# A fused attention and SwiGLU kernel: work behind group 0's first blocks ordered from a job list, more products by sevens

## The chip, the cores and the metric

The kernel runs on one core of one Trainium2 chip. The metric is device time in microseconds (us) from launch to the last store, the median of three runs. TensorE (PE) multiplies matrices into PSUM, a memory of eight banks of 2 KB a partition; VectorE (DVE) and ScalarE (ACT) read and write PSUM and SBUF; GpSimd (POOL) and SyncE (SP) issue the DMAs here.

## The reference

```python
# B, H, S, D = 8, 8, 576, 64; x is 4608 x 512; w_gate, w_val 512 x 1536; w_out 1536 x 512
theta = pi / 2 * arange(S) / S
phi = lambda x: concat([relu(x) * cos(theta), relu(x) * sin(theta)], -1)
kv = einsum('bhsf,bhsd->bhfd', phi(k), v); z = phi(k).sum(axis=2)
attn = einsum('bhsf,bhfd->bhsd', phi(q), kv) / (einsum('bhsf,bhf->bhs', phi(q), z) + 1e-6)
x = attn.transpose(0, 2, 1, 3).reshape(4608, 512)
out = (silu(x @ w_gate) * (x @ w_val)) @ w_out
```

Linear attention without a mask, whose output goes straight into a gated feed-forward layer. All inputs and the output are float32.

## The kernel before

The 4608 tokens are 36 tiles of 128, and nine groups (tg 0 to 8) of 512 tokens. The hidden width 1536 is twelve blocks of 128 (fc 0 to 11). Attention of later batches runs among the feed-forward work of earlier groups.

*Attention.* Loads are issued on POOL (L149), some behind a small copy (a hold) that keeps the queue until a tile is there. For a batch from 2 on, relu and the tables give the features of q (L301) and the weighted v (L311), SP transposes q's features in two DMAs (`phit`, L330), PE makes kv (L361) into a pair of banks, and DVE and ACT take it out (L387, L393). A tile of x (`a_tile2`, L492) is eight products into a pair of banks; then DVE computes den (L506), rec (L515) and x (L519) from both banks. Tiles 4 to 8 are computed as two half tiles (`a_half`, L542): PE fills a pair of banks, ACT makes `tmp` (L552) from both, DVE `num` (L553) from both and tmp. x is transposed by an SP DMA (L596), tiles 6 and 7 by PE.

*Feed-forward.* A plain block (`ffn_fc`) is four 512-column products for the gate and four for val (L612), silu on ACT (L618) and the product of both on DVE (L623). In groups 5 to 8 (`GATE`) the gate is computed for four blocks at a time (a unit u = 0, 1, 2) by seven products of half size in place of eight, after Strassen and Winograd (`ffn_by_quarters`, L670), from weight sums (L645) and sums of x (L653); ACT copies two partial results (L699, L703) and DVE adds two (L709, L718). The out product of groups 1 to 8 is made by seven products in the same way (`out_by_quarters`, L846 with L859 to L887), from sums of tokens (L818) and of weights (L809). Group 0's out product is plain (L787), in pieces of four 512-column products.

*Order.* Every engine works in the order in which its instructions were written. That order is a list of words up to group 0's early blocks, and behind it a plan of slots filled by hand from tables (`ROW`, `TILES`, `LATER`, `LATE`). PSUM is one tile of eight banks; `take(n)` gives one bank or two, a pair being neighbours:

```python
b0 = sorted((b for b in free if b + 1 in free), key=lambda b: max(used[b:b + 2]))
bs = [b0, b0 + 1]
return banks[:, bs[0]] if n == 1 else banks[:, bs[0]:bs[0] + 2]
```

Waits between engines are derived when the kernel is built from what each instruction reads and writes.

Of the kernel before, what the change touches and what calls it, by code (L numbers as in the profile page):

```python
# [18 lines left out]
def kernel(  # L19
# [10 lines left out]
    nc = tc.nc  # L30
# [21 lines left out]
    GATE = (5, 6, 7, 8)  # L52
    AHEAD = 5
    WSUM = (31, 38, 48, 64)
    ROW = {2: ([16, 16, 17, 17], 18, (20, 21, 21, 22), 8), 3: ([12, 12, 14, 14], 18, (17, 20, 21, 21), 6), 4: ([12, 12, 12, 14], 14, (15, 16, 17, 18), 5), 5: ([12, 12, 12, 14], 15, (14, 16, 16, 17), 4), 6: ([6, 8, 11, 12], 12, (13, 14, 15, 18), 3), 7: ([6, 6, 7, 7, 8, 8, 9, 9, 10, 10, 11, 11, 12, 12, 13, 13, 14, 14], 16, (12, 13, 14, 15), 3)}
    TILES = {2: (0, 9, 10, 11), 3: (5, 9, 10, 11), 4: (5, 7, 9, 11), 5: (3, 4, 7, 9), 6: (0, 2, 5, 7), 7: (0, 1, 5, 7), 8: (0, 3, 5, 7)}
    SECOND = (31, 37, 38, 79)
    TSUM = [(2, 2), (2, 3), 18, 19]
    KVONE = (2, 4, 5)
    LATER = {2: (0, 1, 3, 4, 7, 8), 3: (0, 1, 3, 4, 7, 8), 4: (0, 1, 3, 4, 7, 8), 5: (0, 1, 3, 4, 7, 8), 6: (0, 1, 3, 4, 7, 8), 7: (0, 1, 3, 4, 7, 8), 8: (0, 1, 3, 4, 7, 8)}  # L60
    LATE = dict(M=44, V=87, O=131, X=26, x=150, v=(190, 250, 120, 150), e=130, a=90, c=170, b=110, k=120)

    consts = ctx.enter_context(tc.tile_pool(name="consts", bufs=1))
    raw = ctx.enter_context(tc.tile_pool(name="raw", bufs=2))
# [3 lines left out]
    xp = ctx.enter_context(tc.tile_pool(name="xp", bufs=4))  # L68
    xtp = ctx.enter_context(tc.tile_pool(name="xtp", bufs=3))
    smp = ctx.enter_context(tc.tile_pool(name="smp", bufs=3))  # L70
    sgp = ctx.enter_context(tc.tile_pool(name="sgp", bufs=5))
    sg2p = ctx.enter_context(tc.tile_pool(name="sg2p", bufs=3))
    m7p = ctx.enter_context(tc.tile_pool(name="m7p", bufs=2))
    obp = ctx.enter_context(tc.tile_pool(name="obp", bufs=2))
# [10 lines left out]
    filled = [False] * 8  # L85
    loose = [False]
    picks = [0]
    rows = [0]

    def take(n, hold=None, fills=False, seeded=False):  # L90

        taken = {x for r in held.values() for x in r}
        if loose[0]:
            free = [b for b in range(8) if b not in taken]
            picks[0] += 1
            other = picks[0] in SECOND
            if n == 1:
                bs = sorted((b for b in free if filled[b] or not seeded), key=lambda b: used[b])
                bs = bs[min(other, len(bs) - 1):][:1]
            else:  # L100
                b0 = sorted((b for b in free if b + 1 in free), key=lambda b: max(used[b:b + 2]))
                b0 = b0[min(other, len(b0) - 1)]
                bs = [b0, b0 + 1]
            if hold is not None:
                held[hold] = bs
            for b in bs:
                filled[b] = fills or seeded
            touch(bs)
            return banks[:, bs[0]] if n == 1 else banks[:, bs[0]:bs[0] + 2]
        free = [b for b in range(0, 8, n) if not any(b <= x < b + n for x in taken)  # L110
                and (filled[b] or not seeded)]

        b0 = min(free, key=lambda b: (n == 1 and hold is not None and hold[0] == "o" and b ^ 1 not in taken,
                                      sorted(used[b:b + n], reverse=True)))
        if hold is not None:
            held[hold] = range(b0, b0 + n)
        filled[b0:b0 + n] = [fills or seeded] * n
        touch(range(b0, b0 + n))
        return banks[:, b0] if n == 1 else banks[:, b0:b0 + n]

    def touch(r, late=1):
        now[0] += 1
        if loose[0]:
            for x in r:
                used[x] = rows[0] + late
            return
        for x in r:
            used[x] = now[0]

    def give_back(hold, late=1):  # L130
        touch(held.pop(hold), late)


    raws = {}
# [5 lines left out]
    def raw_of(b, nm):  # L140
        if (b, nm) not in raws:
            raws[b, nm] = (rawq if nm == "q" else raw).tile([P, G, NC, D], BF16, name=f"raw_{nm}")
        return raws[b, nm]
# [151 lines left out]
    def phi_q(b, g):  # L295

        if g == 0:
            st[b, "q"] = rel.tile([P, G, NC, 2, D], BF16, name="r_q")
        o = raws[b, "q"][:, g]
        relu_op("act", o, o)  # L300
        nc.vector.tensor_tensor(out=st[b, "q"][:, g], in0=o.unsqueeze(2).to_broadcast([P, NC, 2, D]),  # L301
                                in1=tab, op=ALU.mult)

    def phi_q_part(b, c, w):
        if (b, "q") not in st:
            st[b, "q"] = rel.tile([P, G, NC, 2, D], BF16, name="r_q")
        nc.scalar.activation(out=st[b, "q"][:, :, c, w], in_=raws[b, "q"][:, :, c], func=AF.Relu,
                             scale=csk[:, c, w:w + 1])

# [17 lines left out]
    def qturn_dma(b, e):  # L327
        if e == 0:
            phit[b] = phip.tile([P, 2, G, NC, SH], BF16, name="phit")
        nc.sync.dma_start_transpose(  # L330
            out=phit[b][:, e].rearrange("p g c s -> p (g c) s"),
            in_=st[b, "q"][e * SH:(e + 1) * SH].rearrange("p g c w d -> p (g c w d)"),
        )

# [8 lines left out]
    def qturn_pe(b, j, lo, hi, eng):  # L343
        ps = take(1).bitcast(BF16).rearrange("p (c x) -> p c x", x=P)
        for c in range(lo, hi):
            nc.tensor.transpose(out=ps[:, c - lo], in_=st["qp"][:, b, c, j], identity=ident)
        copy_op(eng, qt_of(b)[:, :, j, lo:hi].rearrange("p e c s -> p c e s"),
                ps[:, 0:hi - lo].rearrange("p c (e s) -> p c e s", e=2))

    def kv_mm(b):  # L350
        if b in KVONE:
            ps = st[b, "kvps"] = [take(1, ("kv", b, e)) for e in range(2)]
        else:
            both = st[b, "kvps"] = take(2, ("kv", b))
            ps = [both[:, e] for e in range(2)]
        for j, c in [(j, c) for j in range(J) for c in range(NC)]:
            for i in range(2):
                for e in range(2):
                    es = slice(e * SH, (e + 1) * SH)
                    g = 2 * j + i  # L360
                    nc.tensor.matmul(  # L361
                        out=ps[e][i * D:(i + 1) * D, j * 2 * D1:(j + 1) * 2 * D1],
                        lhsT=raws[b, "k"][es, g, c],
                        rhs=v2s[b == 1][es, g, c, :, 0:D1],
                        start=(c == 0), stop=(c == NC - 1),
                    )

    def kv_out(b, engs=("act", "dve"), js=slice(0, J)):
        ps = st[b, "kvps"]
        for e, eng in enumerate(engs):  # L370
            for i in range(2):
                hs = slice(i * D, (i + 1) * D)
                (nc.scalar.copy if eng == "act" else nc.vector.tensor_copy)(
                    out=kvd[b % 2][hs, e, js, :, i].rearrange("p j w x -> p (j w) x"),
                    in_=ps[hs, e, js.start * 2 * D1:js.stop * 2 * D1].rearrange("p (y x) -> p y x", x=D1))

    behind = []
    kv2s = [consts.tile([P, 2, J, 2, D1], BF16, name=f"kv2_{j}") for j in range(2)]

    def kv_out2(b):  # L380

        if b in KVONE:
            for e, eng in enumerate((nc.scalar.copy, nc.vector.tensor_copy)):
                ps = st[b, "kvps"][e][:, 0:4 * J * D1 // 2].rearrange("p (j w x) -> p j w x", j=J, w=2)
                for w in range(2):
                    for i in range(2):
                        eng(out=kv2s[b % 2][w * D:(w + 1) * D, e, :, i], in_=ps[i * D:(i + 1) * D, :, w])  # L387
                give_back(("kv", b, e))
            return
        ps = st[b, "kvps"][:, :, 0:4 * J * D1 // 2].rearrange("p e (j w x) -> p e j w x", j=J, w=2)  # L390
        def part(w, eng):
            for i in range(2):
                eng(out=kv2s[b % 2][w * D:(w + 1) * D, :, :, i], in_=ps[i * D:(i + 1) * D, :, :, w])  # L393

        part(0, nc.scalar.copy)
        if b - 1 in GATE:
            behind.append(lambda: (part(1, nc.vector.tensor_copy), kv_free(b)))
        else:
            part(1, nc.vector.tensor_copy)

    def kv_free(b):
        give_back(("kv", b), LATE["k"])

    def kv_first(j, lo=0, hi=NC):

        if lo == 0:
# [96 lines left out]
    def x_den(t, ps, ys=slice(0, 4)):  # L503
        if ys.start == 0:
            st["den", t] = smp.tile([P, H, 1], FP32, name="den")
# [655 lines left out]
```

## Time and profile before

| what | value |
|---|---|
| time, median of 3 runs | 311.84 us (311.62 to 312.58) |
| span of the profiled execution | 309.8 us; its own time is not given apart, the median lies 2.04 us above the span |
| TensorE busy | 302.2 us of the span, mean granted clock 0.999 |
| DVE, ACT, POOL busy | 240.9, 155.5, 67.7 us |
| groups 0 to 8 end at about | 54, 86.6, 119, 151.3, 183.9, 215.4, 246.7, 276.4, 305.2 us |
| from group 8's last product to the end | 4.6 us |

A share of the span is an average. The windows, busy time of each engine between two moments, show it group by group. The list of waits says for how long an engine stood still before an instruction, and which engine's instruction released it. In a timeline the figure in square brackets at a line's end is the idle time before it.

### The profile page before, as it was taken

Reading aid. Unit: us, or ns where it says so; the run is one execution under the profiler, and the core shown is the slowest. Engines: PE = TensorE matmul, PEld = TensorE weight load, DVE = VectorE, ACT = ScalarE, POOL = GpSimd, SP = SyncE. Lnnn points to the kernel's source line nnn. Section 1 sums busy time; section 2 is a strip of 40 time slices with the busy share of each in tenths; the row PEclk is TensorE's granted clock in tenths of the full one; section 3 lists DMA queues with packets and bytes.
Section 4 is the critical chain, followed back from the end, with each engine's and each line's share of the span. In section 5 each row is a group of like instructions: output and inputs, shape, how many; then the busy total and the mean of one; then the engine's idle time right before and its main releaser. Section 6 shows DMA issues by size and latency. Waiting matters only on the chain.

```text
span 309.8 us, 7026 instructions
## 1 busy us (share of the span) xinstructions
PE 302.2 (98%) x2804; PEld 200.5 (65%) x2804; DVE 240.9 (78%) x486; ACT 155.5 (50%) x297; POOL 67.7 (22%) x119
## 2 busy tenths in 40 slices
PE   8899999999999999999999999999999999999993
PEld 4587465445855486547654686768766876786683
DVE  7874678999877988687888887898789569855782
ACT  7454646674355355435644455778553345324530
POOL 7755202001250306030413032202300130031000
PEclk9999999999999999999999999999999999999999
DMA  7999998996499899949696999991991051013005
GB/s 264 222 198 197 206 205 142 227 139 110 72 221 186 129 172 146 202 70 196 123 191 85 200 122 142 126 167 22 179 133 31 14 140 35 19 47 91 0 0 139
DMA packets 72977, 41.10 MB, mean 133 GB/s; under 512 B 49904, under 2 KB 69872, under 8 KB 72944
## 3 DMA queue, kind: packets, MB, share of 16 engines
q0 software_dynamic: 24880, 24.91, 47.0%
q1 hardware_dynamic: 47616, 15.34, 30.8%
q8 instruction: 22, 0.36, 0.5%
q10 hardware_dynamic: 448, 0.39, 0.4%
q14 instruction: 11, 0.09, 0.1%
HBM read 37.75 MB, written 9.44 MB: 152 GB/s over the span
## 4 chain that ended last, share of the span: by engine, by line
PE 92%; DVE 5%; ACT 2%; issue 1%; DVEq 0%; ACTq 0%
PE banks L612 31%; PE banks L846 24%; PE banks L683 13%; PE banks L670 12%; PE banks L787 3%; PE banks L492 2%; PE banks L361 2%; DVE v L311 1%; PE banks L542 1%; PE banks L473 1%; PE banks L215 1%; DVE ht L623 1%; PE banks L416 0%; PE banks L584 0%; ACT L247 0%
## 5 line engine op out<-in xcount | busy, mean ns | idle before, releaser
L618 ACT ACTIVATE sg<-banks 128x512 bf16<-128x512 f32 (+2 forms) x68 | 37.2, 548 | 49.8 <-PE banks L612 49.3
L612 PE MATMUL banks<-xT,wg_sb 128*128 128x512 f16 (+2 forms) x272 | 62.0, 354 | 0.0
L612 PE MATMUL banks<-xT,wv_sb 128*128 128x512 f16 (+2 forms) x272 | 62.0, 354 | 0.0
L623 DVE TENSOR_TENSOR ht<-sg,banks 128x512 f16<-128x512 bf16 (+2 forms) x68 | 41.7, 621 | 17.7 <-PE banks L612 11.8
L769 POOL DMA_DIRECT2D out_dram<-ob x56 | 29.5, 534 | 101.0 <-ACT ob L859 99.2
L683 PE MATMUL banks<-xT,wv_sb 128*128 128x512 f16 x192 | 48.6, 379 | 0.0
L612 PEld LDWEIGHTS <-wv_sb 128*128 128x128 f16 x272 | 26.1, 98 | 26.1
L846 PEld LDWEIGHTS <-ht 128*128 128x128 f16 x384 | 37.4, 98 | 5.4
L612 PEld LDWEIGHTS <-wg_sb 128*128 128x128 f16 x272 | 24.9, 98 | 21.4
L688 DVE TENSOR_TENSOR ht<-sg,banks 128x512 f16<-128x512 bf16 x48 | 31.0, 681 | 3.3 <-ACT sg L676 3.1
L846 PEld LDWEIGHTS <-sums 128*128 128x128 f16 x288 | 28.2, 98 | 3.3
L683 PEld LDWEIGHTS <-wv_sb 128*128 128x128 f16 x192 | 18.8, 98 | 13.3
L676 ACT ACTIVATE sg<-banks 128x512 bf16<-128x512 f32 x36 | 20.5, 590 | 11.8 <-PE banks L670 11.8
L846 PE MATMUL banks<-wo_sb,ht 128*128 128x256 f16 x192 | 23.6, 273 | 0.0
L519 DVE TENSOR_TENSOR x<-banks,rec 128x512 f16<-128x512 f32 (+1 forms) x32 | 21.6, 675 | 1.3 <-PE banks L473 0.3
L670 PEld LDWEIGHTS <-wgs_sb 128*128 128x128 f16 x192 | 17.8, 98 | 7.4 <-issue 0.6
L846 PE MATMUL banks<-wt_sb,ht 128*128 128x256 f16 x192 | 22.3, 273 | 0.0
L846 PE MATMUL banks<-wt_sb,sums 128*128 128x256 f16 x192 | 22.3, 273 | 0.0
L670 PE MATMUL banks<-kvt,wgs_sb 128*128 128x256 f16 x144 | 21.6, 273 | 0.4 <-DVE x L519 0.4
L311 DVE TENSOR_TENSOR v<-raw_v,tab 128x1152 bf16<-128x1152 bf16 x27 | 19.8, 754 | 0.4 <-ACT raw_v L909 0.4
L859 ACT ACTIVATE ob<-banks 128x512 f32<-128x512 f32 x15 | 9.0, 598 | 21.9 <-PE banks L846 21.9
L301 DVE TENSOR_TENSOR r_q<-raw_q,tab 128x1152 bf16<-128x1152 bf16 x20 | 14.4, 754 | 5.1 <-ACT raw_q L284 4.7
(126 smaller groups left out, 411.8 us busy)
## 6 DMA issues: line engine op xcount, KB each, us to landing
out_dram<-ob POOLq DMA_DIRECT2D x56, 128.0 KB, 4.8
raw_k<-in_k_dram POOLq DMA_DIRECT2D x7, 576.0 KB, 6.7
raw_q<-in_q_dram POOLq DMA_DIRECT2D x6, 576.0 KB, 9.0
raw_v<-in_v_dram POOLq DMA_DIRECT2D x6, 576.0 KB, 9.6
wo_sb<-in_moe_w_out_dram POOLq DMA_DIRECT2D x3, 512.0 KB, 12.8
out_dram<-ob SPq DMA_DIRECT2D x12, 128.0 KB, 4.1
wg_sb<-in_moe_w_gate_dram POOLq DMA_DIRECT2D x5, 256.0 KB, 9.0
wv_sb<-in_moe_w_val_dram POOLq DMA_DIRECT2D x5, 256.0 KB, 9.2
```

Source lines behind the costliest of these rows:

```text
L301: nc.vector.tensor_tensor(out=st[b, "q"][:, g], in0=o.unsqueeze(2).to_broadcast([P, NC, 2, D]), in1=tab, op=ALU.mult)
L311: nc.vector.tensor_tensor(out=v2s[b == 1][:, g, :, :, 0:D], in0=(first if b == 0 and g == 0 else {"v": raw_of(b, "v")})["v"][:, g].unsquee ...
L519: nc.vector.tensor_tensor(out=st["x", t].rearrange("p (y e d) -> p e y d", e=2, d=D)[:, :, ys], in0=ps[:, :, 0:2 * J * D1].rearrange("p e ...
L612: nc.tensor.matmul(out=st["f", tg, fc, lo][i], lhsT=(wg_sb, wv_sb)[i][:, kc, fs], rhs=xT[tg][:, ts, kc], start=(kc == 0), stop=(kc == KC - 1))
L618: nc.scalar.activation(out=sg[:, 0:n], in_=st["f", tg, fc, lo][0], func=AF.Silu, scale=DOWN)
L623: nc.vector.tensor_tensor(out=ht[:, fc, r:r + n], in0=st.pop(("s", tg, fc, lo))[:, 0:n], in1=ps[1], op=ALU.mult)
L670: nc.tensor.matmul(out=to[:, i], lhsT=a[:, c, 2 * u + i], rhs=x[:, :, c], start=first and i == 0 and c == 0, stop=c == KH - 1, skip_group_ ...
L676: nc.scalar.activation(out=gates[u, w][:, :, j * HT:(j + 1) * HT], in_=src, func=AF.Silu, scale=DOWN)
L683: nc.tensor.matmul(out=val[u, i, w], lhsT=wv_sb[:, kc, fc * P:(fc + 1) * P], rhs=xT[tg][:, :, kc], start=(kc == 0), stop=(kc == KC - 1))
L688: nc.vector.tensor_tensor(out=ht[:, fc], in0=gates[u, w][:, i], in1=val.pop((u, i, w)), op=ALU.mult)
L769: (queues or (nc.sync, nc.sync))[e].dma_start(out=out_v[idx // NC, idx % NC][:, cols], in_=ob_of(t)[e * SH:(e + 1) * SH, cols])
L846: nc.tensor.matmul(out=to[i][:, 0] if len(to) == 2 else to[0][:, i], lhsT=a[:, kc, i * P:(i + 1) * P], rhs=b[:, kc], start=first and kc == ...
```

## The change

The prologue, the list of words up to group 0's block 5, stays. All work behind it is written as jobs: each has the engines that can do it with a cost for each, the jobs that must come first, and the buffers ("rooms") that it takes and gives back. `order_once` places the jobs one by one when the kernel is built, by earliest start and rank, and the jobs are then emitted in the order of their start. With it:

- The gate is computed by seven products in groups 2 to 8, and val too in groups 7 and 8, for all three units; the sums of val's weights lie where raw k and v lay.
- A unit's gate products are placed among the val products of the unit before it.
- A room of two banks may be any two free banks; the instruction sees them as one view with a step.
- Rotating buffers became fixed ones (9 for silu's output, 3 for the partial sums m7, 4 for x, 2 each for num, tmp and the output).
- Tile 5 is transposed by PE like 6 and 7; kv from batch 2 on is taken out by ACT alone; phit's and xT's transposes on SP come in another order.

New lines of the same steps: plain block L827, L834, L842; products of gate and val L892; plain val L967, L973; out by seven L1059; half tile L677, tmp L689, num L693; tile L735, den L745, rec L750, x L754; kv L617; copies L570, L574; plain out L1167. The core of the diff:

```diff
-    GATE = (5, 6, 7, 8)
+    GATE = set(range(2, NTG))
+    VAL = {(tg, u) for tg in (7, 8) for u in range(3)}
...
+    def bank(r):
+        if r.n == 1:
+            return banks[:, r.at[0]]
+        lo, hi = sorted(r.at)
+        return banks[:, lo:hi + 1:hi - lo]
...
+    def half_tile_jobs(t, key, after, by_pe=False):
+        for jj in range(2):
+            r, tmp = Room("bank", 2), Room("tmp")
...
+            mm = pe(420 if split else 240, fn, (key[0], key[1] + 0.02 * jj), after=after(jj), get=[r] if jj else [r, num])
...
+            def av(r):
+                return bank(r)[:, :, 0:4 * D1].rearrange("p e (w x) -> p e w x", w=2)
...
+            sc_ = Job({"ACT": sc(2 * 130) + 90}, fn, after=[mm], get=[tmp])
...
+            adds.append(Job({"DVE": 410}, fn, after=[sc_], put=[r, tmp]))
...
+    def tile_jobs(t, key):
+        r, x, one_at = Room("bank", 2), Room("x"), Room("tile")
...
+        mm = pe(450 if len(bs) == 2 else 265, fn, key, after=sum((J_["kv", b] + J_["turned", b] for b in bs), []), get=[r, one_at], chore=True)
...
+        def view():
+            return bank(r)[:, :, 0:2 * J * D1].rearrange("p e (y x) -> p e y x", x=D1)
...
+        den = Job({"DVE": 96}, fn, after=[mm], put=[r])
...
+        mul = Job({"DVE": d1(512)}, fn, after=[rec], get=[x], put=[r, one_at])
+        turn_job(t, x, [mul])
...
+    PLAIN = "g1 g3p v0 g7 g6 v2 g2 v1 g5 v3 g4".split()
+    BLOCK = "v1 g3p g1 v7 v6 g7 v2 g6 v5 g2 v4 g5 v3 g4".split()
...
+            for u in range(3):
+                at = places(tg, u)
+                rooms, silus = silu_jobs(tg, u, block_jobs(tg, u, "G", gate_order(tg, u)))
+                if (tg, u) in VAL:
+                    order = [at[f"v{n}"] for n in (1, 7, 6, 2, 5, 4, 3)]
+                    block_mul_jobs(tg, u, rooms, silus, block_jobs(tg, u, "V", order))
...
+            for r in j.get:
+                fs = sorted(f for f in free[r.kind] if not r.seeded or is_filled[f[1]])
+                ok = [f for f in fs if f[0] <= t]
+                if r.kind == "bank" and not r.seeded:
+                    ok.sort(key=lambda f: (is_filled[f[1]], f[0]))
+                take_ = ok[:r.n]
...
+                r.at = [f[1] for f in take_]
...
+    end = order_once(times)
+    best = (end,)
+    for j in sorted(jobs, key=lambda j: j.start):
+        j.fn(j)
```

## The prediction

> **What bounds the kernel now.** I read the page's busy shares first, then the windows by token group, then the waits of TensorE, then the timeline at two places that the change touches.
>
> ```profile
> PE 302.2 (98%) x2804; PEld 200.5 (65%) x2804; DVE 240.9 (78%) x486; ACT 155.5 (50%) x297; POOL 67.7 (22%) x119
> ...
> PE 92%; DVE 5%; ACT 2%; issue 1%; DVEq 0%; ACTq 0%
> ```
>
> TensorE (PE) is busy 98% and carries 92% of the chain that ended last. The windows show the same stage by stage (columns: length, then busy PE, PEld, DVE, ACT, POOL, granted clock, DMA share, GB/s):
>
> ```profile
> 28.00:54.00 26.00, 25.95 (x220) 13.73 (x219) 19.42 (x46) 13.88 (x27) 5.67 (x8) 1.00 1.19 185
> 86.60:119.00 32.40, 32.40 (x294) 19.60 (x292) 26.35 (x48) 15.41 (x29) 8.12 (x15) 1.00 0.96 164
> 183.90:215.40 31.50, 31.08 (x322) 23.07 (x320) 26.88 (x51) 22.16 (x46) 5.86 (x12) 1.00 0.85 117
> 305.20:309.80 4.60, 0.00 (x0) 0.00 (x0) 0.37 (x1) 0.00 (x0) 0.00 (x0) 0.92 0.51 140
> ```
>
> PE has no idle in a plain-gate group (32.40 of 32.40) and 0.42 in group 5, the first with the gate by seven products. So saved PE work is saved time, and every new PE wait is lost time. All waits of PE for another engine are four:
>
> ```profile
> PE banks L215 <- DVE zeros L210: 1.0, 1, 1.0
> PE banks L448 <- DVE wgs_sb L440: 0.7, 1, 0.7
> PE banks L473 <- DVE wt_sb L461: 0.6, 1, 0.6
> PE banks L670 <- DVE x L519: 0.4, 1, 0.4
> ```
>
> The last is the only one behind group 0. Third, group 0's end, where half tiles (L542) stand between pieces of the out product (L787):
>
> ```profile
> 43.95 0.20 DVE L564 RECIPROCAL rec<-den 128x8 f32<-128x8 f32 x1
> 44.16 0.39 PE L542 MATMUL banks<-kvt,phit 128*128 128x260 bf16 x2
> ...
> 44.38 1.03 PE L787 MATMUL banks<-wo_sb,ht 128*128 128x512 f16 x4
> 44.58 0.48 ACT L552 ACTIVATE tmp<-banks,cs_all 128x260 f32<-128x260 f32 x1 [1.43 <-PE banks L542]
> ...
> 45.09 0.49 DVE L553 SCALAR_TENSOR_TENSOR num<-banks,cs_all,tmp 128x260 f32<-128x260 f32 x1
> ```
>
> tmp and num empty the half tile at 44.58 to 45.58 while the piece runs 44.38 to 45.24: beside it, not after it. Last, what a true wait costs:
>
> ```profile
> 189.89 0.20 DVE L515 RECIPROCAL rec<-den 128x8 f32<-128x8 f32 x1
> ...
> 190.13 0.69 DVE L519 TENSOR_TENSOR x<-banks,rec 128x512 f16<-128x512 f32 x1
> ...
> 190.87 0.60 PE L670 MATMUL banks<-kvt,wgs_sb 128*128 128x256 f16 x4 [0.42 <-DVE x L519]
> ```
>
> PE starts 0.05 us after x ends. With 0.2 from the end of a product to its reader, den 0.16, rec and the steps between, a PE product that must wait for a whole tile's den, rec and x costs about 1.4 us; for den alone 0.2 + 0.16 + 0.05 = 0.41.
>
> **The change, PE work.** A 512-column matmul paces 0.216 us (four in 0.864) and a 256-column one 0.1093 (84 in 9.18). Counted in the built order, 512-column matmuls fall from 624 to 384 (240 x 0.216 = 51.8 off), 256-column ones of gate and val rise from 336 to 756 (420 x 0.1093 = 45.9 on), four more transposes of x on PE cost 0.2. Net **-5.7 us**: 3.55 from the gate in groups 2 to 4 and 2.36 from val in 7 and 8, less 0.2. The windows agree: 32.3 to 32.6 for a plain-gate group, 31.5 and 31.3 for groups 5 and 6. Before's own gaps (0.22 at 41.6, 0.58 at 190.3) may go as well: -0.8.
>
> **The helpers' work.** A group that turns to seven products adds 6 DVE adds of 0.604 pitch, 6 ACT copies of 0.51 and four half-width sums of 0.34; group 5 carries this already at DVE 26.9 and ACT 22.2 of 31.5. Val adds 12 more DVE adds in groups 7 and 8, whose DVE has 7 to 9 us free (22.7 of 29.7, 19.8 of 28.8). The val weight sums are 4 x 0.87. Evacuating kv on ACT alone takes a few 0.38 from DVE. Nothing of this sets the end if PE stays gapless; DVE at 86% only means that it catches up slowly after a delay. The prologue (to fc 5 of group 0) and the 4.6 us tail are unchanged: 0.
>
> **Queues.** SP's transposes are reordered: later phit pairs stand between xT transposes, and hold steps and loads move on POOL. A phit pair lands 10.5 to 17.5 us after its first issue in before; tiles 13 and 18 now stand 13.4 to 14.4 us of PE work behind theirs. A lateness of 0 to 2 us each; I take 1 in all, since delays ahead of them push the tiles later too. v of batch 2 at kv: 0 to 0.9, I take 0.4. The last val product of group 8 is followed at once by products on its result: 0.6.
>
> **Banks.** This decides. Before, a two-bank room is always two neighbours. After, the job list gives any two free banks, and the instruction addresses them as one view with a step (`banks[:, lo:hi+1:hi-lo]`): half tiles have [5,7], [0,4], [1,6], [0,7], [1,4]; tiles [2,5], [1,3], [0,7], [2,6], [0,5]; kv pairs [1,6], [1,5]. In the built order I followed each wait to the instruction that it waits for. In after, 150 waits join two instructions that share no bank, and in all 150 the one's bank lies inside the other's span: 37 on PE, 60 on DVE, 53 on ACT. In before PE has none. So den of a pair [0,7] waits for whatever product was issued just before, in any bank, and the next product waits for den, and for x.
>
> Priced at group 0's end (37.9 to 50.8 us of PE's own work; the clock is some 5 us later): a piece in bank 2 ends; 0.2 later num of [0,4] runs (0.48), then tmp of [1,6] (0.48), and only then may the piece in bank 5 start: 0.2 + 0.48 + 0.03 + 0.48 + 0.05 = 1.24. Eleven such places, with what half products fill in: 0.3, 0.3, 1.27, 0.5, 1.26, 1.0, 0.5, 0.7, 0.25, 1.2, 0.75 = **8.0**. Nothing hides it, since PE's next products in order are behind the wait.
>
> At tiles and kv, same coordinate: 62 to 70, 1.4; 82.1 [0,7], 1.4; 90 to 95, 0.9; 118.5 [0,7], 1.6; 124.2 [0,7], 1.35; 149 to 154 (kv [1,6], tiles [2,4], [3,7]), 2.5 to 3.5; 173 to 183, 1.05; 212 to 215, 0.5; 233.9 [0,5], 1.35; to 243, 1.4: **13.5 to 14.5** if each is paid in full. The places where the wait stands on both sides of the pair, which no slack can absorb, make 9.5 of it. Bounds for all bank waits: above, 22.5 plus the 2.0 of queues and tail, 24.5; below, 17.5 from the hard places alone and nothing else. Were the waits always met in time, they would cost 0 to 1.5. I take 18, near the hard sum, because a PE that stalls lets ACT and DVE catch up for the softer places.
>
> The row for the clock: 0 to 10 us has PE busy 8.31 of 10 in pieces, at a granted clock of 1.00, and the 0.58 gap at 190.3 left 1.00 too. So I add nothing for the clock. The Trainium skill (TensorE: Matmul & The Clock Gate, A second HAM failure mode) warns that frequent micro-idles between groups of matmuls can make the gate oscillate; by that, the 13 us of group 0's end at half clock would be 13 us more, about 336. The Trainium skill (PSUM — Partial Sum Buffer, PSUM bank collisions raise a hardware error) asks only for a guard by bank and quadrant; by that, none of the 150 waits is needed, and the sum would be the first rival's. The program as built has them.
>
> **Sum.** Against the profiled execution, span 309.8 with 2.04 around it to the median of 311.84 (its own total is not given, so I take 311.84): 311.84 - 5.7 - 0.8 + 18 = 323.3. Rounded, **323**.
>
> **Rivals.**
> *Waits met in time.* The same 150 waits exist, but their targets are done before PE comes to them, as tmp and num are beside the piece at 44.58. Then 311.84 - 5.7 - 0.8 + 1.5 = 306.8, faster. For it: DVE is idle 4 to 6 us a group, ACT half the time. Against: den and num themselves are held until the product just ahead has ended, so they can't be early. It decides below 6.5 us of waiting in all, where the sum turns to faster. Chance 0.15; time 304 to 311.
> *Only one stretch pays.* Group 0's 8.0 alone gives 311.84 - 6.5 + 8.0 = 313.3; tiles' 9.5 alone 314.8. For it: the tile places depend on how DVE's queue stands, group 0's don't. Against: both have the same cause. Chance 0.12; 311 to 316, mostly slower, hardly any within 0.3%.
> *More than the waits.* DVE, at 86% and made to wait 60 times for products in banks that it doesn't read, falls behind on adds and muls, and banks come free late: some 5 to 8 us more, 328 to 335. Chance 0.15.
> *Forecast.* Chance 0.58; own range 316 to 330.
>
> **Numbers.** 0.3% (0.94 us) is about what this measurement can tell from no change. Faster by more, below 310.9: the first rival, and a little of the second, 0.16. Within: 0.03. Slower: 0.81. A range of 309 to 331 leaves out the lower half of the first rival (0.08) and the top half of the third (0.07) and holds the unknown terms' bounds (17.5 and 24.5 give 322.8 and 329.8). The slower cases hold most of the chance; the likeliest one's own range is above.
>
> **What would show it.** PE's busy sum should fall to about 296.5 while the span grows to about 321. In the waits of PE new lines should appear: the out pieces of group 0 (L1167) for tmp (L689) and num (L693), some 6 to 8 us; gate, val and out products (L892, L967, L1059) for den (L745) and x (L754), some 6 to 12. The stretch of group 0's end, 26 us in before, should be about 8 longer, with the granted clock at 1.00; groups 7 and 8 about 1 each shorter in PE work. I am wrong if those waits sum below 6.5, if the time lost lies at transposes (phit) or loads, or if DVE is busy over 95% in groups 2 to 6.

## The result: 335.07 us, slower by 7.5%, and the profile after

The changed kernel takes 335.07 us (334.9 to 335.6, four runs) against 311.75 us for the kernel before; the ratio is 1.0749, with a 95% interval of 1.0732 to 1.0765. Slower was forecast, 323 us with a range of 309 to 331; 335 lies above it, and twice as much was lost as forecast (23.3 us against 11.5). The profiled execution has a span of 333.3 us, 23.5 more than before.

The page after, busy time by engine and the chain that ended last:

```profile
PE 303.2 (91%) x2988; PEld 218.0 (65%) x2988; DVE 253.7 (76%) x517; ACT 173.6 (52%) x335; POOL 66.9 (20%) x119
...
PE 77%; DVE 9%; DMA 6%; ACT 5%; issue 1%; DVEq 0%; ACTq 0%
```

PE's share of the chain falls from 92% to 77%, and DMA, absent before, has 6%. The longest waits of PE behind the prologue (total, times, longest, us):

```profile
PE banks L1167 <- ACT tmp L689: 1.9, 3, 1.2
PE banks L892 <- DVE kvt L865: 1.9, 1, 1.9
PE banks L1059 <- DVE x L754: 1.6, 2, 1.3
PE banks L892 <- DVE x L754: 1.6, 2, 0.8
PE banks L892 <- DVE den L745: 1.6, 5, 0.4
PE banks L967 <- DVE x L754: 1.6, 3, 0.9
PE banks L677 <- DVE num L693: 1.4, 2, 1.1
PE banks L735 <- DVE x L754: 1.4, 3, 0.5
PE banks L1167 <- DVE num L693: 1.4, 2, 0.9
```

Before had one line behind the prologue (0.4). Out, gate and val products wait for den, x, tmp and num, which read banks that these products don't write: as built, 127 waits join two instructions without a bank in common, and in each the one's bank lies inside the other's span. Group 0's end in the timeline:

```profile
43.80 1.02 PE L1167 MATMUL banks<-wo_sb,ht 128*128 128x512 f16 x4 [0.16 <-ACT tmp L689]
...
44.93 0.49 DVE L693 SCALAR_TENSOR_TENSOR num<-banks,cs_all,tmp 128x260 f32<-128x260 f32 x1 [0.77 <-PE banks L1167]
45.46 0.48 ACT L689 ACTIVATE tmp<-banks,cs_all 128x260 f32<-128x260 f32 x1 [1.71 <-DVE num L693]
45.99 1.02 PE L1167 MATMUL banks<-wo_sb,ht 128*128 128x512 f16 x4 [1.16 <-ACT tmp L689]
```

A piece, then num, then tmp, then the next piece: strictly one after another, 1.16 us idle, where before tmp and num ran beside a piece. At a tile the same in two steps:

```profile
97.41 0.17 DVE L745 TENSOR_SCALAR den<-banks 128x8 f32<-128x8 f32 x1 [0.45 <-PE banks L1059]
...
97.63 0.60 PE L892 MATMUL banks<-kvt,wgs_sb 128*128 128x256 f16 x4 [0.26 <-DVE den L745]
...
98.27 0.69 DVE L754 TENSOR_TENSOR x<-banks,rec 128x512 f16<-128x512 f32 x1 [0.45 <-PE banks L892]
...
99.01 0.38 PE L892 MATMUL banks<-kvt,wg_sb 128*128 128x256 f16 x2 [0.78 <-DVE x L754]
```

den waits for the product just ahead, one product slips in, x waits for that one, and PE waits for x.

To close the account I add up, from 20 us on, by how much the start of each PE product comes later than the pace of the one before allows (0.216 us for 512 columns, 0.109 for 256; excesses over 0.06 counted), under the name of what it waited for; most gaps under 0.15 us stand as unnamed. "Neighbours" and "neighbours, PE turns" are the runs e_near and e_turn below.

| PE stands still for, us | before | after | neighbours | neighbours, PE turns |
|---|---|---|---|---|
| den and x of tiles | 0.6 | 10.8 | 0.9 | 0.7 |
| tmp and num of half tiles | 0 | 7.7 | 0 | 0 |
| kv copies | 0 | 2.7 | 0 | 0 |
| transposes of x, sums of x behind them | 0 | 3.0 | 7.8 | 2.0 |
| transposes of phit | 0 | 0 | 1.8 | 1.2 |
| adds and copies of the seven products, last product | 0 | 2.6 | 1.5 | 2.4 |
| unnamed: between products of unlike shape, short gaps, lowered clock | 1.9 | 4.0 | 3.2 | 2.5 |
| rest | 0.5 | 1.2 | 2.6 | 2.3 |
| all | 3.0 | 32.0 | 17.8 | 10.9 |

From the span of before: 309.8 - 5.7 of PE work + (32.0 - 3.0) = 333.1, measured 333.3. For the neighbours 309.8 - 5.7 + 14.8 = 318.9 (319.2); with turns on PE, 1.8 more work, 309.8 - 3.9 + 7.9 = 313.8 (314.2). The rows are rounded each by itself, so a column can differ from its sum by 0.2. So the saving of 5.7 us is there in full; everything else is standing still. In the neighbours' column some 1.3 us of the unnamed are products at half clock (see the end).

### The profile page after: what moved, and what is told of

Its sections match the earlier page's. It is cut to its first block, busy times and chain, and to the rows that moved or that the text cites. A ratio compares the mean times of both kernels' runs of the same rounds, so it can differ in the third digit from the quotient of the medians.

```text
span 333.3 us, 7436 instructions
## 1 busy us (share of the span) xinstructions
PE 303.2 (91%) x2988; PEld 218.0 (65%) x2988; DVE 253.7 (76%) x517; ACT 173.6 (52%) x335; POOL 66.9 (20%) x119
## 4 chain that ended last, share of the span: by engine, by line
PE 77%; DVE 9%; DMA 6%; ACT 5%; issue 1%; DVEq 0%; ACTq 0%
PE banks L1059 22%; PE banks L892 22%; PE banks L967 12%; PE banks L827 8%; DMA xT<-x 6%; PE banks L416 3%; DVE x L754 3%; PE banks L1167 3%; PE banks L617 2%; PE banks L735 2%; ACT kv L570 2%; DVE num L693 1%; ACT tmp L689 1%; DVE ht L973 1%; PE banks L356 1%
## 5 line engine op out<-in xcount | busy, mean ns | idle before, releaser
L967 PE MATMUL banks<-xT,wv_sb 128*128 128x512 f16 x240 | 60.0, 379 | 2.0 <-DVE x L754 1.6
L951 ACT ACTIVATE sg<-banks 128x512 bf16<-128x512 f32 x63 | 36.5, 592 | 16.8 <-PE banks L892 12.3
L1059 PEld LDWEIGHTS <-ht 128*128 128x128 f16 x384 | 37.3, 98 | 9.1 <-issue 2.9
L973 DVE TENSOR_TENSOR ht<-sg,banks 128x512 f16<-128x512 bf16 x60 | 39.7, 677 | 3.4 <-ACT kv L570 1.4
L892 PEld LDWEIGHTS <-wgs_sb 128*128 128x128 f16 x336 | 32.3, 98 | 15.2 <-issue 6.5
L967 PEld LDWEIGHTS <-wv_sb 128*128 128x128 f16 x240 | 23.2, 98 | 20.8 <-issue 3.2
L892 PE MATMUL banks<-kvt,wgs_sb 128*128 128x256 f16 x216 | 31.3, 272 | 4.6 <-DVE kvt L865 1.9
L892 PEld LDWEIGHTS <-wg_sb 128*128 128x128 f16 x252 | 24.4, 98 | 9.9 <-issue 3.2
L1059 PEld LDWEIGHTS <-sums 128*128 128x128 f16 x288 | 28.0, 98 | 4.0 <-issue 0.6
L951 ACT ACTIVATE sg<-m 128x512 bf16<-128x512 f32 x21 | 13.2, 630 | 30.3 <-DVE m L920 30.3
L1059 PE MATMUL banks<-wo_sb,ht 128*128 128x256 f16 x192 | 26.2, 273 | 2.8 <-DVE x L754 1.6
L892 PE MATMUL banks<-xT,wg_sb 128*128 128x256 f16 x168 | 25.2, 272 | 1.5 <-DMA xT<-x 0.7
L570 ACT COPY banks<-banks 128x512 f32<-128x512 f32 (+1 forms) x36 | 20.1, 567 | 12.0 <-PE banks L1059 8.1
L1059 PE MATMUL banks<-wt_sb,sums 128*128 128x256 f16 x192 | 25.4, 273 | 0.4 <-ACT kv L570 0.4
L912 DVE TENSOR_TENSOR banks<-m,banks 128x512 f32<-128x512 f32 x27 | 18.6, 690 | 8.6 <-ACT m L570 8.2
L754 DVE TENSOR_TENSOR x<-banks,rec 128x512 f16<-128x512 f32 x27 | 18.2, 688 | 7.2 <-PE banks L892 2.8
L1059 PE MATMUL banks<-wt_sb,ht 128*128 128x256 f16 x192 | 22.6, 273 | 0.0
L570 ACT COPY m<-banks 128x512 f32<-128x512 f32 x27 | 15.7, 587 | 8.8 <-PE banks L892 5.2
L827 PE MATMUL banks<-xT,wg_sb 128*128 128x512 f16 x72 | 18.5, 379 | 1.5 <-ACT tmp L689 0.9
L261 DVE TENSOR_TENSOR v<-raw_kv,tab 128x1152 bf16<-128x1152 bf16 x27 | 19.2, 750 | 0.5 <-ACT raw_kv L437 0.5
```

What stands on the lines that cost most here:

```text
L261: nc.vector.tensor_tensor(out=v2s[b == 1][:, g, :, :, 0:D], in0=(first if b == 0 and g == 0 else {"v": raw_of(b, "v")})["v"][:, g].unsquee ...
L570: nc.scalar.copy(out=out, in_=in_)
L754: tt(out=one(x_all, x).rearrange("p (y e d) -> p e y d", e=2, d=D), in0=view()[:, :, :, 0:D], in1=rec_all[:, t % 4].rearrange("p (e y) o - ...
L827: nc.tensor.matmul(out=bank(r), lhsT=w[:, kc, fc * P:(fc + 1) * P], rhs=xT[tg][:, :, kc], start=(kc == 0), stop=(kc == KC - 1))
L892: nc.tensor.matmul(out=to[:, i], lhsT=a[:, c, 2 * u + i], rhs=x()[:, :, c], start=first and i == 0 and c == 0, stop=c == KH - 1, skip_grou ...
L912: tt(out=bank(c), in0=one(m7_all, m).rearrange("p i x -> p (i x)"), in1=bank(b), op=ALU.add)
```

## The experiments

**1. Banks alone (e_near).** The job list's order stays as it is on every engine; only the banks are dealt out anew, under the list's own times, so that every pair is two neighbours (`near` tells which rooms get neighbours, here all).

```diff
+                if r.n == 1:
+                    sets = [(b,) for b in ok]
+                elif near(r):
+                    sets = [(b, b + 1) for b in range(7)]
...
+    near_ = lambda r: True
...
+    for r, s in found[1].items():
+        r.at = s
     for j in sorted(jobs, key=lambda j: j.start):
         j.fn(j)
```

> The changed kernel with every engine's order untouched; only the names of the PSUM banks are dealt anew, so that each pair is two neighbours and no wait joins instructions without a bank in common. Theory (the waits across a pair's span cost the time): of the 32 us that TensorE stands still behind the prologue, the 10.8 put down to den and x, the 7.7 to tmp and num and most of the 2.7 to kv go; about 311 us, range 308 to 314. Rival (the order itself: DVE late with adds and sums, transposes late): the same stops come back under other names, 322 us or more.

Measured 321.49 us (320.67 to 323.27), ratio to before 1.0325 (1.029 to 1.0359): 13.6 us less than with spread pairs, but still some 10 us above the 311 expected. Both theories are half right. The waits for den, x, tmp, num and kv fall from 21.2 to 0.9, so the spread pairs made them. But the waits for transposes grow from 3.0 to 9.6. These are PE's three longest waits (kvt L865 is the sums of x, which lie in kvt's memory):

```profile
PE banks L892 <- DVE kvt L865: 6.0, 2, 4.5
PE banks L735 <- DMA phit<-r_q: 1.6, 1, 1.6
PE banks L892 <- DMA xT<-x: 1.3, 1, 1.3
```

**2. One kind of pair at a time (e_near_half, e_near_rest).** As in experiment 1, but neighbours only for half tiles, or only for tiles and kv; other pairs are two or more banks apart (not the same ones as in the changed kernel). The second run has `not` ahead of `hasattr`.

```diff
+            r.half = True
...
+                else:
+                    sets = [(a, b) for a in range(8) for b in range(a + 2, 8)]
...
+    near_ = lambda r: hasattr(r, "half")
```

> As the run with all pairs as neighbours, but only the half tiles' pairs of group 0 are neighbours; tiles and kv keep pairs two or more apart. Theory: the 7.7 us of tmp and num go, den, x and kv stay: about 326 us (323 to 329). Rival (the order): 333 or more, no change.

> The other half: only tiles and kv have neighbours, half tiles keep pairs two or more apart. Theory: the 7.7 us of tmp and num stay and about 12 go: about 321 us (318 to 325); with the half-tile run the two gains add up to that of all pairs. Rival (the order): 332 or more.

Single runs: 331.7 and 331.12 us, gains of 3.4 and 4.0, where 9 and 14 were expected. In the first, tmp and num are gone (0), but den and x stand at 15.3 and kv at 5.4, since the other spread pairs fell elsewhere. In the second tmp and num are at 6.4 and the transposes, phit's among them, at 10.8. So the two gains can't be added: both runs have other spread pairs than the changed kernel, and in the second the transposes take back 7.8 us (10.8 against 3.0) of what the other waits give free.

**3. Spread pairs in the kernel before (b_far).**

```diff
-                b0 = sorted((b for b in free if b + 1 in free), key=lambda b: max(used[b:b + 2]))
+                b0 = sorted((b for b in free if b + 2 in free), key=lambda b: max(used[b:b + 3:2]))
...
-                bs = [b0, b0 + 1]
+                bs = [b0, b0 + 2]
...
-            return banks[:, bs[0]] if n == 1 else banks[:, bs[0]:bs[0] + 2]
+            return banks[:, bs[0]] if n == 1 else banks[:, bs[0]:bs[0] + 3:2]
```

> The kernel before with one edit: from group 1 on a pair of banks is b and b+2 in place of b and b+1, the order of every engine unchanged. Theory: nine waits of TensorE across a pair's span appear; at 0.4 to 1.4 us each 4 to 9 us are lost: 316 to 321 us. Rival (the spread pair is harmless, it is the new order that loses): 312 us, within 1 us of before.

326.12 us, ratio 1.0456 (1.0439 to 1.0474): 14.5 us lost by this alone, over twice the middle of what was expected. No engine's order differs from before. PE's longest waits:

```profile
PE banks L670 <- DVE x L519: 8.6, 7, 1.9
PE banks L683 <- DVE x L519: 1.4, 1, 1.4
PE banks L683 <- DVE kv L393: 1.3, 1, 1.3
```

And what one of them is made of, on DVE and PE:

```profile
222.24 0.70 DVE L709 TENSOR_TENSOR banks<-m,banks 128x512 f32<-128x512 f32 x1 [0.95 <-PE banks L670]
222.85 0.16 DVE L506 TENSOR_SCALAR den<-banks 128x8 f32<-128x8 f32 x1
223.04 0.20 DVE L515 RECIPROCAL rec<-den 128x8 f32<-128x8 f32 x1
223.28 0.69 DVE L519 TENSOR_TENSOR x<-banks,rec 128x512 f16<-128x512 f32 x1
```

```profile
224.02 0.83 PE L670 MATMUL banks<-xT,wg_sb 128*128 128x256 f16 x4 [1.89 <-DVE x L519]
```

den comes behind an add (L709) that itself had waited for a product, so PE pays add, den, rec and x: 1.89 us idle, not 1.4.

**4. Why are the transposes late? (e_land, e_own)** With the neighbours kept: longer landings in the list (a landing is the time from a DMA's issue to its data being there), or each group's first gates at its own start. From here on the list orders the jobs anew in every run, so that more changes than the lines shown.

```diff
-    X_LAND = 5200.0
-    PHI_LAND = 9500.0
+    X_LAND = 9000.0
+    PHI_LAND = 14000.0
...
-            turned.append(Job({"SP": 3700}, fn, after=phis + J_.get(("tiles", b - 2), []), tail=PHI_LAND - 3700))
+            turned.append(Job({"SP": 5300}, fn, after=phis + J_.get(("tiles", b - 2), []), tail=PHI_LAND - 5300))
```

> Pairs as neighbours, and the job list told of longer transposes: a tile of x lands 9.0 us after its issue in place of 5.2, a half of phit 14.0 in place of 9.5 and holds SP's queue 5.3 in place of 3.7; the jobs are ordered anew. Theory A (what is left of the loss, 9.6 us of waits for transposes, comes from landing times set too short when the order was made): these waits fall below 3 us, 311 to 315 us. Rival B (gates a unit ahead across a group's border need x too early, whatever landing is set): the waits stay or move, 319 us or more.

```diff
+        if not u:
+            return [(tg - 1, 3.96 + 0.005 * n) for n in range(7)]
```

> Pairs as neighbours, and the first unit's gate products of a group stand at the group's own start, behind the out products of the group before, in place of the last unit of the group before; the other units stay a unit ahead. Rival B: x is wanted some 15 us later, the waits for transposes vanish and TensorE waits for the first sigmoids instead by 0 to 1 us a group: 311 to 316 us. Theory A: no gain, 319 to 324 us.

e_land took 325.63 to 334.34 us over four runs, above theory A's range in each. In the profiled run, one of 332.20 us, the waits for x's transposes did fall to 1.9, but one new wait of 11.8 us stands at 102 us; how long it was in the run of 325.63 no trace shows. The cause in the profiled run: ACT's queue held a relu on k, whose load had not landed, ahead of the silu that PE needed.

```profile
111.08 2.40 ACT L249 ACTIVATE raw_kv<-raw_kv 128x576 bf16<-128x576 bf16 x4 [12.87 <-DMA raw_kv<-in_k_dram]
113.39 0.61 ACT L951 ACTIVATE sg<-m 128x512 bf16<-128x512 f32 x1
```

e_own took 324.63 us (ratio 1.0413, 1.0394 to 1.0431), 3 us more than with the gates ahead: no wait for x's transposes is left, as rival B had it, but 7.0 us for an ACT copy (L570), of which two, 2.5 and 3.2 us, are the bulk; ahead of the first, ACT waits 1.54 us for k's load, and ahead of the second 4.61 us for q's:

```profile
112.06 2.40 ACT L249 ACTIVATE raw_kv<-raw_kv 128x576 bf16<-128x576 bf16 x4 [1.54 <-DMA raw_kv<-in_k_dram]
150.99 1.83 ACT L249 ACTIVATE raw_q<-raw_q 128x576 bf16<-128x576 bf16 x3 [4.61 <-DMA raw_q<-in_q_dram]
```

Both theories miss the time, theory A by 0.6 us. What they have in common is seen in experiment 1's trace: DVE and ACT work in order, and an instruction whose transfer is late holds all behind it.

```profile
144.68 0.69 DVE L1010 TENSOR_TENSOR ht<-ht 128x1024 f16<-128x1024 f16 x1
150.65 0.76 DVE L865 TENSOR_TENSOR kvt<-xT 128x512 f16<-128x512 f16 x2 [5.29 <-DMA xT<-x]
151.33 0.42 DVE L865 TENSOR_TENSOR kvt<-xT,kvt 128x512 f16<-128x512 f16 x1
151.66 0.68 DVE L973 TENSOR_TENSOR ht<-sg,banks 128x512 f16<-128x512 bf16 x1
```

The last transpose of x awaited here was issued at 138.57 and landed at 150.63; three loads and a phit were under way in this time. That these slowed it is likely, but no run has it apart.

**5. What the extra products are worth (e_noval, e_gate5).** Neighbours, and `VAL = set()`; then also `GATE = set(range(5, NTG))`, the same products as in the kernel before.

> Pairs as neighbours, val plain in all groups. TensorE has 2.36 us more to do. If groups 7 and 8 are bound by TensorE, 323 to 325 us; if val's extra adds and copies cost there what they save, 321 us or less.

> Pairs as neighbours, the gate by seven products in groups 5 to 8 only and val plain, as in the kernel before, but ordered from the job list. TensorE has 5.9 us more to do than with all of it. If the late transposes of groups 2 to 4 come from the sums of x that the seven products need early, about 10 us of waits go and the time is 316 to 320 us; if the order from the job list loses by itself, 325 us or more. Were the order as good as the one by hand: 312 us.

e_noval: 324.71 us (ratio 1.042, 1.0399 to 1.0441), 3.2 more than with val by sevens: in groups 7 and 8 the products pay, about their 2.36 us of PE work. e_gate5: 322.05 us (1.0334, 1.0308 to 1.036), between the first two of the expected ranges. It does before's PE work and stands still 13.6 us instead of 3.0; transposes of x no longer appear, but ACT and DVE are late with evacuations (ACT and DVE waits of 3.8 us for q, 3.5 and 2.6 for phit stand in their queues). So the list's order stands still 10.6 us longer than the one by hand at the same products, and 14.8 us longer (17.8 against 3.0) with the extra ones. That is the order with all that came with it, the fixed buffers and kv taken out by ACT alone among it; no run has these apart.

**6. Transposes taken off the DMA (e_turn).** Neighbours, and:

```diff
-        turn_job(t, x, [mul])
+        turn_job(t, x, [mul], 12 <= t < 20, (key[0], key[1] + 0.06))
```

> Pairs as neighbours, and the eight tiles of groups 3 and 4 are transposed by TensorE in place of an SP DMA (0.22 us of TensorE and one ACT copy of 0.51 each). Theory C (most of what is left comes from transposes that land 8 to 12 us after their issue while loads share the DMA engines, and from sums of x that block DVE until then): the 7.8 us of waits for x in those groups go, 1.8 us of TensorE work come: 314 to 317 us. Rival D (the order from the list is tight everywhere, a wait removed here returns at the next place): 319 to 323 us.

315.23 us (313.76 to 315.99), ratio 1.0101 (1.0072 to 1.013): 6.3 us gained over the neighbours (5.0 by the profiled spans), at the middle of theory C's range. The waits for x fall from 7.8 to 2.0:

```profile
PE banks L892 <- DMA xT<-x: 1.3, 1, 1.3
PE banks L892 <- DVE kvt L865: 0.4, 1, 0.4
```

The order of DVE and ACT is another one here, so the gain as a whole fits theory C, but isn't shown to come from the transposes alone.

**7. Landings set long for the loads (e_loads, g5_late).** Neighbours, `LAND = (12000.0, 13000.0, 14000.0)` in place of `(6500.0, 7500.0, 8500.0)`; g5_late adds this and experiment 4's first edit to e_gate5.

> Pairs as neighbours, and the job list told that the loads of k, v and q land 12 to 14 us after their issue in place of 6.5 to 8.5; ordered anew. Theory C: fewer ACT and DVE instructions stand before work whose data have not landed, waits for loads at the head of ACT's and DVE's queues fall from about 10 us to below 3; but the list then has to leave TensorE idle for the loads, so 318 to 324 us. If the landing times alone were the fault: 312 to 316.

> Pairs as neighbours, gate by seven products from group 5 on only, val plain, and all landing times set long (loads 12 to 14, a tile of x 9.0, half a phit 14.0). If the order from the list loses to the one by hand only by landings that it takes as too short: 312 to 316 us. If the list can't place the transposes and loads early enough in the first place: 322 us or more, with TensorE waiting for kv and tiles.

e_loads took 334.85 and 341.82 us, worse than any expectation: in the profile, of the run of 341.82, ACT's waits for loads of q are 1.7 us against 7.2 with the neighbours, but the sums of x wait 13.6 us for transposes on DVE, against 9.3. g5_late took 328.68 (1.0548, 1.0518 to 1.0579), slow as the second branch of its expectation had it, but PE waits most for silu (3.9) and sums of x (3.0), and only then for x of tiles (2.7). One landing time per kind of transfer, short or long, doesn't fit: with the neighbours a tile's transpose landed 2.4 to 12.1 us after its issue.

**8. Carried on (e_t2v).** e_turn with tiles 12 to 23 on PE, and val plain in the last unit of group 8.

> The best kernel so far (pairs as neighbours, tiles transposed by TensorE) carried on: tiles of group 5 too are transposed by TensorE (12 to 23), and the very last unit of group 8 has val plain, so that its out product needn't wait for the add and product of the seventh result. Theory C: 2.0 us of waits for x in group 5 and about 0.6 to 1.5 at the last out product go, 0.9 + 0.4 us of TensorE work come: 313 to 315 us. Rival D (a wait removed here returns at the next place): 315 to 317 us. Faster than before would be below 311 us.

315.49 us (314.49 to 316.79; ratio 1.0112, 1.0078 to 1.0146), no gain on e_turn beyond the spread of the runs: the waits for x in group 5 went, and one of 2.7 us for a silu (L951) came at 182 us. Rival D fits this step. No version here beats the kernel before; its order by hand with neighbouring pairs stays the fastest, by 3.7 us.

**9. Do the two causes add up? (a_turn)** Experiment 6's edit on the changed kernel, its spread pairs kept.

> The changed kernel with its spread pairs kept, and the eight tiles of groups 3 and 4 transposed by TensorE in place of an SP DMA; nothing else. Theory (the waits across a pair's span come first and hide most of the late transposes): the 3.0 us of waits for x that the changed kernel shows go, 1.8 us of TensorE work come, and new spread pairs may cost a little: 332 to 336 us, where the same edit gave 6.3 us once the pairs were neighbours. Rival (the late transposes are a loss of their own, whatever the pairs): 328 to 330 us.

338.59 us (1.0864, 1.081 to 1.0918): 3.5 us worse than the changed kernel, where the same edit gained 6.3 with neighbours; above both expected ranges. Waits for x fell from 3.0 to 1.7, those for den, x, tmp, num and kv rose from 21.2 to 24.0. So the late transposes cost little while the bank waits stand; experiment 1, where the order stayed, shows the same from the other side (waits for x grow from 3.0 to 7.8 as the bank waits go). And this run and e_turn have the same order on every engine and differ by the banks alone: the spread pairs cost 23.4 us here (338.59 against 315.23).

## Why the prediction was right on the sign and wrong on the size

- *The step that failed* is the 18 us for all that PE would newly wait. PE stands still 32.0 us from 20 us on, 29.0 more than before, and this was foreseen as 18 less 0.8.
- *PE work, -5.7.* Right by the pace: each of the three spans above closes to within 0.5 us with it. What was to show it did not: PE's busy sum rose to 303.2, where 296.5 was foreseen. A row ends later than the pace (four 256-column products show 0.60 us where the pace is 0.44), so each stop adds to the busy time; with neighbours the same products show 299.3.
- *The clock.* Right for the changed kernel, 0.997 granted, and 1.00 at group 0's end (41.9 to 65.5 us). That the 336 put beside it, for half clock there, lies near the 335.07 is chance.
- *The waits exist and cost.* Right, in the places named. Their count was wrong: of the 150 waits, 23 join instructions that do have a bank in common (two readers); 127 join disjoint banks, all of PE's among them.
- *Bank waits, "I take 18, near the hard sum".* This is the first mis-sized term. They measured 21.2, close to the upper end of 22.5; the hard sum, 17.5, was too low. Group 0's end was right: 8.0 foreseen, 7.7 for tmp and num. Tiles and kv cost 13.5 (10.8 and 2.7), the low end of what was worked out "if each is paid in full", where 9.5 for the hard places was taken. So the reason given, that a stalled PE lets ACT and DVE catch up for the softer places, is what failed. Why they don't is only argued: they wait for PE's products too, as num does at 44.93, and 1.4 us for den, rec and x left out what else DVE has in front of them; experiment 3 shows 1.89 with an add ahead.
- *Queues, "I take 1 in all".* The second, and in kind the greater miss. Of the 2.0 worked out for queues and tail, the 18 holds only 0.5. The transposes watched were phit's; those that cost were x's, 3.0 us, because gate products read the sums of x (L865), which wait in DVE's order for these transposes. With neighbours they are 7.8, so the first rival's 306.8, which had no term for it, was out of reach too: without the bank waits the kernel takes 321.5.
- *The helpers' work, put at 0 "if PE stays gapless".* The third. PE isn't gapless, and waits for adds and copies of the seven products cost 2.0 of the 2.6 (the last product's 0.6 was foreseen). Not in the sum at all were the unnamed stops, 4.0 against 1.9 before, part of them short waits.
- The account: 32.0 against 18 is 14.0 more. Bank waits make 3.7 of it (21.2 against 17.5), all other rows 10.3 (3.0, 2.6, 4.0 and 1.2, less the 0.5 that the 18 held for them). Before's own standing still gives 2.2 back (3.0 against the 0.8 taken off), and 11.8 is left, as 335.1 against 323.3.
- *The third rival*, DVE behind and banks late, 328 to 335, came nearest in time and had 0.15. DVE isn't the bound, though: it is busy 76%. It stands behind waits, so the nearness is luck.

## What to carry to other kernels

The builder of these kernels orders a view that steps over PSUM banks against everything inside its span, so give an instruction that reads two banks two neighbours, and price a spread pair by all that its reader's engine has queued. Before moving work on in-order engines by a list, ask of each instruction what transfer it waits for and what stands behind it, since one late transfer holds up evacuations that have nothing to do with it. Waits in series hide each other: take the largest away and measure again before adding up the rest.

## What the runs showed of the hardware

The changed kernel stood still 32 us in pieces of at most 2.1 us, and the mean granted clock was 0.997. In e_near one gap of 4.48 us before 151.47 us was followed by half clock (windows of 2 us; the granted clock is the third figure from the end):

```profile
150.00:152.00 2.00, 0.53 (x3) 0.41 (x4) 1.35 (x4) 1.26 (x2) 0.00 (x0) 0.72 1.25 249
152.00:154.00 2.00, 2.00 (x12) 1.38 (x10) 2.00 (x5) 1.46 (x3) 0.00 (x0) 0.50 0.84 139
```

In b_far three gaps of 1.89 us are alike, and one of them, before 224.02, was followed by 0.56 and 0.59 in the next two windows of 2 us, while those before 188.48 and 262.01 left 1.00. What sets that one apart is open. The Trainium skill (TensorE: Matmul & The Clock Gate, A second HAM failure mode) has the clock oscillate with frequent micro-idles between groups of products; the changed kernel's 0.997 doesn't show that. What its section on HAM oscillation says, that idle beyond a window of about 3.4 us brings the clock down, agrees with the gap of 4.48 us here; the 1.89 us in b_far is shorter than that window, and the clock fell all the same.
